# Score tiles by halves of the heads, an earlier second batch, and constants off VectorE, in an attention kernel that feeds a mixture of experts

## The chip, the cores and the metric

The kernel runs on one core of one Trainium2 chip. The metric is the device time of one execution in microseconds (us), the median of several runs. TensorE (PE in the profile) multiplies matrices and writes to PSUM, VectorE (DVE) and ScalarE (ACT) work on tiles element by element, GpSimd (POOL) does the same and issues indirect DMAs, SyncE (SP) issues most of the loads and stores. Each engine takes its own instructions in order and waits on semaphores for the others.

## The reference

Eight batches, eight heads, 512 tokens and 32 states per head, head size 64; then a mixture of eight experts over all 576 rows of a batch, with hidden size 1024.

```python
B, H, S, Ns, D = (8, 8, 512, 32, 64)
scores = scale * np.matmul(x, state.transpose(0, 1, 3, 2))
a = softmax(scores)                          # over the states
xread = np.matmul(a, state)
scores2 = scale * np.matmul(state, x.transpose(0, 1, 3, 2))
a2 = softmax(scores2)                        # over the tokens
sread = np.matmul(a2, x)
x = concat([xread, sread], axis=2)           # to (B, 576, 512)
...
logits = x @ w_gate
local_gate = sigmoid(x @ w_local)
for b, s in rows in order:
    e = argmax(logits[b, s]) if s == 0 or local_gate[b, s] < 0.5 else prev_e
    prev_e = e
    out[b, s] = softmax(logits[b, s])[e] * (relu(x[b, s] @ w1[e]) @ w2[e])
```

Everything is float32 from input to output.

## The kernel before

The kernel has three stages: the attention of the eight batches, the routing (which expert takes which row, and where in the sorted order it goes), and the experts.

In the attention one batch is one round of some 30 steps, each a small method of `Attention`. The steps of all batches are interleaved in one list written out by hand, `STEPS`: a step is two letters and the digits of its arguments (`sc3` is the scores of batch 3, `tr21` a transpose for batch 2, tile 1). They are issued in that order, and each engine runs its own share in that order. `go` ends a piece of the list; the steps behind the first `go` are used as filling between the parts of the routing.

Of a batch, x is held twice: transposed (`x_t0` and `x_t1`, two tiles of 128 x 1024, loaded in two halves by steps `xt`) and with tokens on partitions (`x_n`, step `xn`). Three batches of each fit. The states are held transposed in `sttc` (batch 0 in a tile of its own, batches 1 to 7 in another), and plain in `states_of`, from which four steps `sd` make block-diagonal tiles in `sd`.

Step `sc` (`scores`, L311 to L313) computes the scores of one batch as two PSUM tiles `s`, u = 0 and u = 1, of 128 x 512: on partitions 32k to 32k + 31 of tile u stand the 32 states of head 2k + u. A head takes 64 rows of contraction. So a batch has 8 matmuls of 64 rows x 32 columns x 512 tokens. In before the contraction of tile u lies on partitions 64u to 64u + 63, and k = 0, 1 use `x_t0`, k = 2, 3 use `x_t1`. Behind it: `mx` (maximum over tokens on VectorE), `nb` (scaled on GpSimd), `et` (exponents over tokens on ScalarE), `tr` (32 x 32 transposes of a score tile on VectorE), `mo`, `sb`, `ex`, `zh`, `zs`, `zi`, `ml` (softmax over states, on VectorE, GpSimd and ScalarE), `tb` (turned back on VectorE), `tu` and `ec` (TensorE transposes of the exponents, L383, and their copies), `sr` (state reads, L396), `st`, `rt`, `sl`, `sk` (their logits, L416), `lg` and `lt` (token logits, L428), `vv` (token reads, 2 matmuls each, L438), `xr` and `wr` (copied by ScalarE, L444, and written to the DRAM tensor `rows`, L452). `ga` and `gl` multiply the states with the gate weights (L295). `kp` and `wm` are matmuls on zeros that keep TensorE's clock up (L266, L306).

`Routing.constants` and `Routing.more_constants` make index tables ahead of the attention: iotas on GpSimd, casts on ScalarE, comparisons and memsets on VectorE. `Attention.clear` sets buffers to zero on GpSimd between the two.

The routing begins with the last batch's logits and is mostly one chain on VectorE; the experts multiply by a seven-product scheme on TensorE.

Of the kernel before, what the change touches and what calls it, by code (L numbers as in the profile page):

```python
# [8 lines left out]
F32 = mybir.dt.float32  # L9
I32 = mybir.dt.int32  # L10
BF16 = mybir.dt.bfloat16
# [145 lines left out]
sc0 kp3 xt11 xt10 mx00 ga kp2 sd3 tr01 xt21 mx01 sd2 mo01 nb0 tr00 et01 sb01 xn0 mo00 wm14 sc1 et00 sb00 ex01  # L157
iv0 tu01 tr11 gl tu00 zh01 ex00 tr10 xt20 ec00 zh00 zs01 mo10 sd0 xn1 zs00 sb10 zi0 ec01 mx11 sd1 sr0 ml01 mo11
ex10 mx10 sc2 ml00 st0 xt30 tb01 rt0 sb11 tb00 sl0 xt31 tr20 lg0 nb1 ex11 zh10 sk0 tr21 vv03 et10 zh11 xt41 zs10
vv00 et11 lt0 mx21 xr03 xt51 zs11 tu11 zi1 xr00 tu10 iv1 ml11 mo21 vv02 xt50 ec10 mo20 ml10 sc3 ec11 tb11 xt40  # L160
xr02 mx20 sb21 sr1 tb10 xn2 tr30 sb20 ex21 lg1 mx30 st1 vv12 zh21 ex20 rt1 tr31 nb2 sl1 zh20 et20 vv10 zs21 sk1
lt1 ws1 zs20 et21 tu20 zi2 xt60 mo30 xr10 ml20 sc4 xr12 iv2 mx31 ec20 xn3 ml21 tu21 tb20 vv11 mx41 ec21 nb3 sb30
et30 tb21 sr2 tr40 et31 xt61 lg2 mo31 ex30 tu30 mo40 sb31 st2 sc5 lt2 wr00 xr11 mx40 ec30 zh30 tr41 wr03 tu31
ex31 nb4 zs30 sb40 vv23 et40 mx50 xt70 ec31 mo41 tu40 zh31 ex40 rt2 sr3 sb41 zs31 ws0 xr23 zi3 xn5 et41 iv3 sl2
ml31 mx51 vv22 ex41 sk2 iv4 st3 ml30 tb31 sc6 xr22 rt3 ec40 zh41 tb30 xt71 sl3 zh40 zs41 lg3 tr50 nb5 vv31 wr02
zs40 et50 zi4 vv01 xn4 lt3 xr31 ml40 mo50 sk3 tr51 xr01 vv13 ml41 tb40 et51 vv21 mo51 sb50 xr13 wr10 iv5 vv20
tb41 xr21 sb51 xn6 mx60 ex50 lg4 mx61 xr20 zh50 tu50 ex51 lt4 tu41 tr60 nb6 ec50 zh51 tu51 zs50 et60 mo60 vv32
wr20 ec51 zs51 sb60 zi5 tu60 ec41 wr23 tr61 sc7 xr32 ml50 wr11 ex60 mo61 sr4 et61 ml51 tb50 wr12 mx71 sr5 sb61
ws2 st4 tb51 ec60 ws3 vv30 tr70 zh60 ex61 xn7 mx70 st5 lg5 zh61 xr30 zs60 tu61 mo70 nb7 et70 vv40 zs61 sb70 zi6
ec61 tu70 lt5 wr22 iv6 xr40 ml61 rt5 sr6 rt4 ex70 tr71 wr40 ec70 ml60 mo71 sl5 et71 wr13 sl4 sk5 tb61 vv41 sb71  # L170
st6 wr31 tb60 tu71 zh70 ex71 sk4 iv7 wr32 lg6 rt6 xr41 zs70 zh71 sl6 ec71 lt6 wr21 vv42 zs71 zi7 wr01 sr7 sk6
xr42 ml71 ch0 ch1 wr42 vv33 st7 ml70 wr41 vv50 tb71 xr33 rt7 wr33 sl7 tb70 ch2 xr50 sk7 wr30 wr50 lg7 vv53 xr53 lt7
wr53 vv51 go xr51 wr51 go vv43 xr43 wr43 vv52 xr52 wr52 ws4 go vv61 xr61 wr61 ws5 go vv60 xr60 wr60 vv62 xr62 wr62
vv71 ws7 go xr71 wr71 ws6 go vv72 go xr72 wr72 vv63 xr63 wr63 vv70 xr70 wr70 vv73 xr73 wr73
# [3 lines left out]
class Attention:  # L178


    def __init__(self, ctx, tc, p, late, xn, xt, st, stt, wgl, wgs, lt, rows, none):
# [14 lines left out]
        self.sttc = [once.tile([P, n, KT, N], F32, name=f"sttc{i}") for i, n in enumerate((1, B - 1))]  # L196
# [5 lines left out]
        nc.sync.dma_start(out=self.sttc[1], in_=stt[:, 1:])  # L202
# [82 lines left out]
    def states(self, b):  # L285
        return self.sttc[b > 0][:, b - (b > 0)]

    def gates(self):
        nc = self.nc
        self.ws = [self.bank() for u in range(G)]  # L290
        for u, w in enumerate(self.ws):
            r = slice(64 * u, 64 * u + 64)
            for b in range(B):
                for k in range(KT):
                    nc.tensor.matmul(w[32 * k:32 * k + 32, b * (E + 1):(b + 1) * (E + 1)],  # L295
                                     lhsT=self.states(b)[r, k, :], rhs=self.wh[r, k, :], start=True, stop=True)
# [11 lines left out]
    def scores(self, b):  # L308
        s = [self.new(self.sp, "s", (b, u), [P, S], tag="s") for u in range(G)]
        for k in range(KT):  # L310
            for u in range(G):  # L311
                r = slice(64 * u, 64 * u + 64)
                self.nc.tensor.matmul(s[u][32 * k:32 * k + 32, :], lhsT=self.states(b)[r, k, :],  # L313
                                      rhs=self.get(f"x_t{k // 2}", b)[r, k % 2, :], start=True, stop=True)
# [140 lines left out]
class Routing:  # L455
# [6 lines left out]
    def constants(self, ident):  # L462
# [6 lines left out]

        ci = rt.tile([P, B, NC], I32, name="ci")  # L470
# [14 lines left out]
        self.raw = pi, ci, iof, iob, identb, place  # L485

    def more_constants(self):
        nc, rt = self.nc, self.rt
        pi, ci, iof, iob, identb, place = self.raw
# [4 lines left out]
        before = rt.tile([P, P], BF16, name="before")  # L494
        nc.vector.tensor_scalar(before, iob, part, None, Alu.is_gt)
# [5 lines left out]
        nc.vector.tensor_scalar(ev.rearrange("p e o -> p (e o)"), iof[:, :E], 1.0, None, Alu.add)  # L501
        up = self.up = rt.tile([P, 1, E], F32, name="up")
        nc.vector.tensor_scalar(up[:, 0], iof[:, :E], 1.0, None, Alu.add)
# [862 lines left out]
```

## Time and profile before

| | us |
|---|---|
| median of 3 runs (523.31 to 524.8) | 524.16 |
| the profiled execution | 524.12 |
| its span | 522.3 |
| PE busy | 508.6 (97%) |
| DVE busy | 297.9 (57%) |
| POOL busy | 268.3 (51%) |
| ACT busy | 180.8 (35%) |

The page of the profile lists busy times, then the chain of work that ended last (followed back from the last instruction, at each step to what released it), then groups of instructions with the mean time of one and the idle time ahead of them. A row of a timeline gives start, length, engine, line, operation, `output<-inputs`, sizes and the number of instructions merged in it; in brackets stands the idle time ahead and what ended it. A row of a table of stretches gives its bounds, its length, the busy time of PE, PEld (weight loads), DVE, ACT and POOL with the number of instructions, the granted clock of TensorE, the share of the DMA engines and GB/s. The granted clock is 1.00 in all rows shown here.

### The profile page before, as it was taken

The page shows a single profiled execution, that of the slowest core. Times are in us where ns is not written, and L with a number is a line of the kernel's source. Part 1 is how long each engine was busy: PE and PEld are TensorE (multiplying, and loading weights), DVE is VectorE, ACT ScalarE, POOL GpSimd, SP SyncE. Part 2 cuts the span into 40 slices and gives each one's busy share as a digit, 9 for nine tenths or more (in the row PEclk, how much of TensorE's full clock was granted, in tenths as well). Part 3 has the DMA queues.
Part 4 walks back from the last instruction along what each step waited for, and adds up shares of the span by engine and source line. Part 5 has one row for each costly group of instructions (what it writes and reads, how often), then busy time and mean ns, then how long its engine had stood idle before and what let it go on. Part 6 is the DMA issues. An engine that isn't in the chain of part 4 may idle for free.

```text
span 522.3 us, 10537 instructions
## 1 busy us (share of the span) xinstructions
PE 508.6 (97%) x4028; PEld 423.3 (81%) x4028; DVE 297.9 (57%) x514; ACT 180.8 (35%) x381; POOL 268.3 (51%) x333
## 2 busy tenths in 40 slices
PE   8799999999999999999999999999999999999995
PEld 3557776988888888888888888888888888888884
DVE  5999986989516750684067416661475256715401
ACT  7797755332232322331232222321331232222321
POOL 7788803774663663564474655564554566012002
PEclk9999999999999999999999999999999999999999
DMA  8999777996646815945914964913962947350001
GB/s 318 411 328 399 264 254 217 302 373 232 238 163 214 319 61 207 382 167 178 386 62 139 405 219 142 405 60 124 384 270 73 407 160 229 134 199 25 2 21 67
DMA packets 38142, 116.76 MB, mean 224 GB/s; under 512 B 5425, under 2 KB 6577, under 8 KB 34754
## 3 DMA queue, kind: packets, MB, share of 16 engines
q1 hardware_dynamic: 30866, 98.03, 50.7%
q0 software_dynamic: 7072, 17.90, 10.3%
q8 instruction: 34, 0.56, 0.4%
q14 instruction: 26, 0.21, 0.1%
q10 hardware_dynamic: 144, 0.07, 0.0%
HBM read 98.14 MB, written 17.89 MB: 222 GB/s over the span
## 4 chain that ended last, share of the span: by engine, by line
PE 89%; DMA 4%; DVE 2%; POOL 1%; issue 1%; ACT 1%; SPq 0%; POOLq 0%; DVEq 0%
PE ps L1104 22%; PE ps L1160 21%; PE sum L1104 16%; PE sum L1160 15%; PE p L438 4%; DMA x_t<-in_xt_dram 3%; PE ps L985 3%; PE ps L973 3%; PE s L313 1%; PE p L396 1%; PE p L383 1%; PE ps L735 1%; PE ps L559 1%; DMA y<-rows,four 1%; PE p L428 1%
## 5 line engine op out<-in xcount | busy, mean ns | idle before, releaser
L891 POOL DMA_INDIRECT xg<-rows,row x112 | 126.9, 1133 | 29.6 <-issue 26.5
L1104 PE MATMUL ps<-xt,a 128*128 128x256 f32 (+1 forms) x400 | 91.5, 372 | 0.1
L1104 PE MATMUL sum<-xs,a 128*128 128x256 f32 x376 | 88.7, 379 | 0.0
L1104 PEld LDWEIGHTS ps<-xt,a 128*128 128x128 f32 x400 | 73.3, 190 | 11.3 <-issue 1.8
L1104 PEld LDWEIGHTS sum<-xs,a 128*128 128x128 f32 x376 | 71.4, 190 | 9.7
L1088 POOL DMA_INDIRECT out_dram<-y,tok x32 | 35.1, 1096 | 83.9 <-DVE y L1176 43.6
L999 DVE TENSOR_TENSOR h<-s,s 128x512 f32<-128x512 f32 x16 | 11.1, 695 | 91.2 <-ACT s L1138 91.2
L1160 PE MATMUL ps<-c,h 128*128 128x256 f32 x264 | 63.0, 381 | 0.0
L1160 PE MATMUL ps<-c,hs 128*128 128x256 f32 x256 | 60.5, 379 | 0.0
L904 POOL COPY tick<-s 1x1 f32<-1x1 f32 x72 | 22.9, 318 | 70.5 <-ACT s L1165 45.7
L1160 PE MATMUL sum<-c,h 128*128 128x256 f32 x248 | 58.6, 379 | 0.0
L1160 PEld LDWEIGHTS ps<-c,h 128*128 128x128 f32 x264 | 49.7, 190 | 8.6 <-issue 2.1
L1160 PEld LDWEIGHTS ps<-c,hs 128*128 128x128 f32 x256 | 48.6, 190 | 6.6
L1160 PEld LDWEIGHTS sum<-c,h 128*128 128x128 f32 x248 | 47.1, 190 | 6.4
L999 DVE TENSOR_TENSOR a<-a,a 128x1024 f32<-128x1024 f32 x32 | 37.7, 1215 | 5.8 <-DMA a<-in_w_dram 5.4
L999 DVE TENSOR_TENSOR c<-c,c 128x1024 f32<-128x1024 f32 x32 | 37.6, 1215 | 2.8 <-DMA c<-in_w_dram 2.6
L438 PE MATMUL p<-sd,a 128*128 128x256 f32 x128 | 32.4, 390 | 0.2 <-ACT xr L444 0.2
L1104 PE MATMUL ps<-xs,a 128*128 128x256 f32 x136 | 32.0, 379 | 0.0
L1138 ACT COPY s<-sum 128x512 f32<-128x512 f32 x32 | 18.7, 585 | 37.5 <-PE sum L1104 37.5
L999 DVE TENSOR_TENSOR y<-s,s 128x256 f32<-128x256 f32 x16 | 6.8, 423 | 42.9 <-ACT s L1165 42.9
L1160 PE MATMUL sum<-c,hs 128*128 128x256 f32 x128 | 30.2, 379 | 0.0
L1165 ACT ACTIVATE s<-sum,prob 128x256 f32<-128x256 f32 x32 | 15.2, 474 | 42.7 <-PE sum L1160 42.7
(226 smaller groups left out, 699.7 us busy)
## 6 DMA issues: line engine op xcount, KB each, us to landing
at<-in_w_dram SPq DMA_DIRECT2D x18, 1024.0 KB, 7.7
ct<-in_w_dram SPq DMA_DIRECT2D x18, 1024.0 KB, 10.2
a<-in_w_dram SPq DMA_DIRECT2D x32, 512.0 KB, 5.0
c<-in_w_dram SPq DMA_DIRECT2D x32, 512.0 KB, 10.0
x_t<-in_xt_dram SPq DMA_DIRECT2D x16, 512.0 KB, 11.2
x_n<-in_xn_dram SPq DMA_DIRECT2D x8, 1024.0 KB, 9.6
rows<-xr SPq DMA_DIRECT2D x32, 256.0 KB, 4.4
xg<-rows,row POOLq DMA_INDIRECT x112, 4.7
```

Source lines behind the costliest of these rows:

```text
L313: self.nc.tensor.matmul(s[u][32 * k:32 * k + 32, :], lhsT=self.states(b)[r, k, :], rhs=self.get(f"x_t{k // 2}", b)[r, k % 2, :], start=Tru ...
L438: self.nc.tensor.matmul(v[:, d], lhsT=self.get("a", b, u)[:, c * P:c * P + P], rhs=self.sd[:, b, d], start=True, stop=True)
L891: nc.gpsimd.indirect_dma_start(out=to.rearrange("p x k -> p (x k)"), out_offset=None, in_=rows.rearrange("n q x -> (n q) x"), in_offset=ba ...
L904: nc.gpsimd.tensor_copy(tick, value)
L973: nc.tensor.matmul(hps[SQ * g:SQ * g + SQ, :], lhsT=self.x_t[:, j, :], rhs=a[:, j, :, g], start=(j == 0), stop=(j == KT - 1))
L985: nc.tensor.matmul(yps[SQ * g:SQ * g + SQ, :], lhsT=self.h[:, m, :], rhs=ct_[:, 2 * m // FK, g // 2, m % (FK // 2), g % 2 * P:g % 2 * P + ...
L999: nc.vector.tensor_tensor(out, a, b, op=op)
L1088: put = nc.gpsimd.indirect_dma_start(out=out, out_offset=to, in_=y, in_offset=None, bounds_check=NT - 1, oob_is_err=False)
L1104: nc.tensor.matmul(to[:, m * width + columns.start:m * width + columns.stop], lhsT=w[:, j, f:f + P], rhs=x[:, j, columns], start=begin and ...
L1138: nc.scalar.copy(to, t)
L1160: nc.tensor.matmul(to, lhsT=x[:, m, n * P:n * P + P], rhs=w[:, m, :], start=begin and m == 0, stop=(m == FK // 2 - 1), skip_group_check=True)
L1165: nc.scalar.activation(to, t, Act.Copy, scale=p)
```

## The change

1. **Scores.** Tile u is now computed whole ahead of the other tile, and its contraction uses both halves of the partitions: matmul k of tile u contracts over partitions 64 (k % 2) to 64 (k % 2) + 63 (`heads`). The layouts of `xt`, `stt` and the gate weights in `kernel` follow, so that `x_t0` holds what tile 0 needs and `x_t1` what tile 1 needs. The result in `s` is the same. `gates` uses the same places.
2. **Loads.** `sttc` is three tiles: batch 0, batch 1, batches 2 to 7. Batch 1's states and its x are issued in the constructor, ahead of the other states and the gate weights.
3. **Constants.** The table `before` (1 where the column is greater than the row) is built by GpSimd (`late`) and cast by ScalarE. `ev` is a ScalarE activation and `up` another view of it. `quarter` is four memsets.
4. **First steps.** The first 62 or so steps of the list stand in another order, and `wm14` is gone; from `ex11` on (the last 362 steps) the list is the same.

```diff
-sc0 kp3 xt11 xt10 mx00 ga kp2 sd3 tr01 xt21 mx01 sd2 mo01 nb0 tr00 et01 sb01 xn0 mo00 wm14 sc1 et00 sb00 ex01
...
+sc0 kp4 mx00 tr00 sd3 mx01 nb0 mo00 sc1 kp3 et00 tr01 sb00 mo01 et01 sb01 xn0 xt20 xt21 tu00 tu01 kp2 ga tr10 mx10
...
-        self.sttc = [once.tile([P, n, KT, N], F32, name=f"sttc{i}") for i, n in enumerate((1, B - 1))]
+        self.sttc = [once.tile([P, n, KT, N], F32, name=f"sttc{i}") for i, n in enumerate((1, 1, B - 2))]
...
-        nc.sync.dma_start(out=self.sttc[1], in_=stt[:, 1:])
+        nc.sync.dma_start(out=self.sttc[1], in_=stt[:, 1:2])
+        for h in range(2):
+            self.load_t(1, h)
+        nc.sync.dma_start(out=self.sttc[2], in_=stt[:, 2:])
         nc.sync.dma_start(out=wgs.rearrange("p w k e -> p (w k e)"), in_=wgl)
...
     def states(self, b):
-        return self.sttc[b > 0][:, b - (b > 0)]
+        return self.sttc[min(b, 2)][:, b - min(b, 2)]
+
+    def heads(self, u):
+        return [(slice(32 * k, 32 * k + 32), KT // 2 * u + k // 2, slice(64 * (k % 2), 64 * (k % 2) + 64))
+                for k in range(KT)]
...
     def scores(self, b):
         s = [self.new(self.sp, "s", (b, u), [P, S], tag="s") for u in range(G)]
-        for k in range(KT):
-            for u in range(G):
-                r = slice(64 * u, 64 * u + 64)
-                self.nc.tensor.matmul(s[u][32 * k:32 * k + 32, :], lhsT=self.states(b)[r, k, :],
-                                      rhs=self.get(f"x_t{k // 2}", b)[r, k % 2, :], start=True, stop=True)
+        for u in range(G):
+            for q, k, r in self.heads(u):
+                self.nc.tensor.matmul(s[u][q, :], lhsT=self.states(b)[r, k, :],
+                                      rhs=self.get(f"x_t{u}", b)[r, k % 2, :], start=True, stop=True)
...
+        late = rt.tile([P, P], F32, name="late")
+        nc.gpsimd.memset(late, 0.0)
+        nc.gpsimd.affine_select(out=late, in_=late, compare_op=Alu.is_ge, fill=1.0, base=0, pattern=[[-1, P]],
+                                channel_multiplier=1)
...
+        before = rt.tile([P, P], BF16, name="before")
+        nc.scalar.copy(before, late)
...
-        nc.vector.tensor_scalar(before, iob, part, None, Alu.is_gt)
...
-        nc.vector.tensor_scalar(ev.rearrange("p e o -> p (e o)"), iof[:, :E], 1.0, None, Alu.add)
-        up = self.up = rt.tile([P, 1, E], F32, name="up")
-        nc.vector.tensor_scalar(up[:, 0], iof[:, :E], 1.0, None, Alu.add)
+        nc.scalar.activation(ev[:, :, 0], iof[:, :E], Act.Relu, bias=1.0)
+        self.up = ev.rearrange("p e o -> p o e")
...
-        nc.vector.tensor_scalar(pi, pi, SQ.bit_length() - 1, None, Alu.logical_shift_right)
         quarter = rt.tile([P, 1], F32, name="quarter")
-        nc.vector.tensor_scalar(quarter, pi, float(Q * NT), None, Alu.add)
+        for i in range(Q):
+            nc.vector.memset(quarter[SQ * i:SQ * i + SQ], float(Q * NT + i))
```

How the instructions stand on three engines, at the start of the program. SP's loads before: `x_t_111` and `x_t_113` are the halves of batch 0, `x_t_227` and `x_t_229` of batch 1, `x_t_304` and `x_t_360` of batch 2; batch 0's states come by another queue.

```order
L279 DMA x_t_111<-in_xt_dram 128x1024
L279 DMA x_t_113<-in_xt_dram 128x1024
L201 DMA states_of<-in_st_dram 128x1024
L202 DMA sttc_109<-in_stt_dram 128x896
L203 DMA wgs<-in_wg_dram 128x72
L279 DMA x_t_227<-in_xt_dram 128x1024
L279 DMA x_t_229<-in_xt_dram 128x1024
L279 DMA x_t_304<-in_xt_dram 128x1024
L283 DMA x_n<-in_xn_dram 128x2048
L279 DMA x_t_360<-in_xt_dram 128x1024
```

And SP's loads now: `x_t_112` and `x_t_114` are batch 0, `x_t_119` and `x_t_121` batch 1, `x_t_275` and `x_t_277` batch 2.

```order
L282 DMA x_t_112<-in_xt_dram 128x1024
L282 DMA x_t_114<-in_xt_dram 128x1024
L201 DMA states_of<-in_st_dram 128x1024
L202 DMA sttc_109<-in_stt_dram 128x128
L282 DMA x_t_119<-in_xt_dram 128x1024
L282 DMA x_t_121<-in_xt_dram 128x1024
L205 DMA sttc_110<-in_stt_dram 128x768
L206 DMA wgs<-in_wg_dram 128x72
L286 DMA x_n<-in_xn_dram 128x2048
L282 DMA x_t_275<-in_xt_dram 128x1024
L282 DMA x_t_277<-in_xt_dram 128x1024
```

Batch 1's x has moved ahead of the states of batches 2 to 7 and of the gate weights; in both orders the same tensors stand up to and with batch 2's last half.

TensorE before, from the gates' last matmuls (on `wgs`) over the scores of batch 1 (`x_t_229`, `x_t_227`), batch 0's transposes (`ident`) and state reads (`x_n`) to batch 2's scores and what follows them:

```order
L313 MATMUL s<-x_t_229,sttc_109 32x512 x4
L313 MATMUL s<-x_t_227,sttc_109 32x512 x4
L383 MATMUL p<-ident,e_312 128x128 x4
L383 MATMUL p<-ident,e_336 128x128 x4
L396 MATMUL p<-x_n,e 32x64 x32
L313 MATMUL s<-x_t_360,sttc_109 32x512 x4
L313 MATMUL s<-x_t_304,sttc_109 32x512 x4
L416 MATMUL p<-wgs,rt 32x9 x4
L428 MATMUL p<-a,gl 32x128 x8
```

The same stretch of TensorE now, without the matmuls on zeros between its pieces:

```order
L320 MATMUL s<-x_t_119,sttc_109 32x512 x4
L320 MATMUL s<-x_t_121,sttc_109 32x512 x4
...
L390 MATMUL p<-ident,e_264 128x128 x4
L390 MATMUL p<-ident,e_270 128x128 x4
...
L303 MATMUL p<-wgs,sttc_110 32x9 x24
...
L403 MATMUL p<-x_n,e 32x64 x32
L320 MATMUL s<-x_t_275,sttc_110 32x512 x4
L320 MATMUL s<-x_t_277,sttc_110 32x512 x4
L423 MATMUL p<-wgs,rt 32x9 x4
```

The gates moved from ahead of batch 1's scores to behind batch 0's transposes. A row of four score matmuls was half of the contractions of both tiles, and is one whole tile now.

VectorE before, from the last of the attention's memsets to batch 0's first maximum (`nb<-s`) and transpose:

```order
L495 TENSOR_SCALAR before<-iob,part 128x128
L497 MEMSET ones 128x128
L499 MEMSET one 1x1
L501 TENSOR_SCALAR ev<-iof 128x8
L503 TENSOR_SCALAR up<-iof 128x8
L510 MEMSET on 128x328
L511 MEMSET on 128x8
L518 TENSOR_SCALAR pi<-pi 128x1
L520 TENSOR_SCALAR quarter<-pi 128x1
L522 MEMSET ex 128x40
L321 TENSOR_REDUCE nb<-s 128x1
L340 STREAM_TRANSPOSE e_302<-s 128x512
```

And the same place of VectorE now:

```order
L508 MEMSET ones 128x128
L510 MEMSET one 1x1
L520 MEMSET on 128x328
L521 MEMSET on 128x8
L530 MEMSET quarter 32x1 x4
L532 MEMSET ex 128x40
L328 TENSOR_REDUCE nb<-s 128x1
L347 STREAM_TRANSPOSE e_240<-s 128x512
```

All five operations that read another tile are gone from it; memsets are left.

More of the change, by code (lines that the diff above doesn't have):

```diff
@@ L162 @@
[L162 to L166, printed above, removed]
@@ L175 @@
+wr73
 """
@@ L484, in constants @@
         self.blocks = blocks
-        self.raw = pi, ci, iof, iob, identb, place
+        before = rt.tile([P, P], BF16, name="before")
+        nc.scalar.copy(before, late)
+        self.raw = pi, ci, iof, iob, identb, place, before
     def more_constants(self):
         nc, rt = self.nc, self.rt
-        pi, ci, iof, iob, identb, place = self.raw
+        pi, ci, iof, iob, identb, place, before = self.raw
         part = rt.tile([P, 1], F32, name="part")
@@ L493, in more_constants @@
         nc.scalar.copy(cols, ci.rearrange("p b i -> p (b i)"))
-        before = rt.tile([P, P], BF16, name="before")
-        nc.vector.tensor_scalar(before, iob, part, None, Alu.is_gt)
         ones = rt.tile([P, P], BF16, name="ones")
```

39 lines of the change are left out of this document (21 added, 18 removed).

## The prediction

> **What bounds the kernel now.** I read the page first (TensorE, PE, is busy 97% of the span), then the chain that ended last, then the table of stretches over the attention, then the instructions of TensorE in order of time, and last the start on VectorE (DVE), GpSimd (POOL) and the loads. The change touches nothing behind the attention except constants, so the question is when the attention ends. The chain of work for its first part reads:
>
> ```profile
> 6.65 11.63 DMA x_t<-in_xt_dram
> 18.28 0.04 issue
> 18.32 1.09 PE s L313 x16
> 19.42 0.36 PE p L416 x8
> 19.78 0.13 issue
> 19.91 0.65 PE p L428 x16
> ...
> 24.22 1.02 PE s L313 x16
> ...
> 29.77 1.02 PE s L313 x16
> ...
> 34.30 1.02 PE s L313 x16
> ...
> 38.07 1.38 issue
> ...
> 41.28 1.02 PE s L313 x16
> ```
>
> The columns are start, length and what ran. Until 18.28 us the end hangs on a load, the third batch's transposed x. From there TensorE follows TensorE. The rows of L313 are the score matmuls of batches 2, 3, 4, 5 and 6; those of batch 7 come at 50.89, in this row of TensorE's timeline:
>
> ```profile
> 50.89 1.09 PE L313 MATMUL s<-x_t,sttc 64*32 64x512 f32 x16
> ```
>
> The table of stretches says whether TensorE has room there (length, then the busy time of each engine):
>
> ```profile
> 18.32:38.07 19.75, 19.60 (x347) 12.85 (x348) 19.04 (x45) 16.34 (x40) 15.65 (x22) 1.00 0.98 355
> 38.07:39.45 1.38, 0.00 (x1) 0.00 (x1) 1.12 (x4) 1.29 (x4) 1.38 (x2) 1.00 1.07 423
> 39.45:61.70 22.25, 22.04 (x425) 16.59 (x424) 20.52 (x53) 18.04 (x43) 19.18 (x25) 1.00 0.91 340
> 61.70:72.40 10.70, 10.49 (x130) 7.97 (x131) 9.37 (x27) 5.63 (x12) 2.75 (x3) 1.00 0.70 258
> ```
>
> PE has 19.60 of 19.75 us, then one hole of 1.38, then 22.04 of 22.25. So from 18.3 to 61.7 us TensorE has 0.36 us of room beside that hole. VectorE is close behind (19.04 and 20.52), but TensorE takes its instructions in order, and whatever is added to it there moves everything behind it. That this is work and not modelled ends is seen from what a record costs, below.
>
> **The score tiles (the main term).** In before, the 8 score matmuls of a batch use 8 different places of the array: rows 0-63 for tile u = 0, rows 64-127 for u = 1, and column group k of 32 for each of the four k. After, both tiles use rows 64*(k%2) and columns 32k: the four matmuls of u = 0 occupy four places, and the four of u = 1 the same four again. The other four stand idle. What does that cost? Batch 0 shows four matmuls alone, twice, since the halves of its x land apart:
>
> ```profile
> 5.48:6.60 1.12, 1.06 (x8) 0.15 (x8) 1.00 1.04 424
> 6.60:7.75 1.15, 1.06 (x8) 0.15 (x8) 1.00 1.01 413
> 18.31:19.42 1.11, 1.09 (x16) 0.18 (x16) 1.00 1.00 406
> ```
>
> These are stretches of L313 alone. An f32 matmul leaves two records; 8 records (four matmuls) take 1.06 us, 16 records (eight) take 1.09. So eight places run side by side, and four are no faster than eight. What one place takes follows from the columns streamed through it:
>
> ```profile
> 20.48 1.99 PE L438 MATMUL p<-sd,a 128*128 128x256 f32 x8
> 23.19 1.03 PE L438 MATMUL p<-sd,a 128*128 128x256 f32 x4
> 25.17 1.10 PE L396 MATMUL p<-x_n,e 128*32 128x64 f32 x64
> ```
>
> L438 fills the array: 4 records of 256 columns, 1024 in all, take 1.03 us, and 8 (2048 columns) 1.99. L396 works in four column groups: 64 records / 4 = 16 of 64 columns each, again 1024, 1.10 us. The scores of before put 2 records of 512 = 1024 columns through each place, 1.09 us. After, each of four places gets 4 records of 512 = 2048 columns, which the L438 row prices at 1.99. That is 1.99 - 1.09 = **+0.90 us a batch**; the bounds are 1.99 - 1.10 = 0.89 and 1.99 - 1.03 = 0.96. The trace of before has no row with two matmuls queued on one 64x32 place, so this is an estimate from L396 and L438.
>
> Which batches pay? Batch 0: its halves already run apart, nothing is added. Batch 1 runs before 18.3, where TensorE waits for loads. Batch 2: its first tile needs only the first half of x, which lands one transfer (512 KB by the row below) before the second; at the 406 to 424 GB/s that end the rows of the stretches above that is 0.52/0.41 = 1.3 us, more than the 1.0 that the first tile takes. So only the second tile, 1.06 us, lies behind the last landing, as 1.09 did: nothing. Batches 3 to 7 pay: 5 x 0.90 = **+4.5 us** (4.45 to 4.8).
>
> ```profile
> x_t<-in_xt_dram SPq DMA_DIRECT2D x16, 512.0 KB, 11.2
> ```
>
> **The loads.** Batch 1's x no longer waits for the states of batches 2 to 7 (128 x 768 f32, 393 KB) nor the gate weights (128 x 72, 37 KB): 0.43 MB at some 0.415 MB/us, 1.0 us earlier. But batch 2's x stands behind exactly the same transfers as before, only in another order. The queues are full until then, and the landing that starts the TensorE stretch stays at 18.28. Worth nothing behind 18.3, by itself.
>
> **Constants and first steps.** VectorE begins late today:
>
> ```profile
> 3.31 3.50 POOL L226 MEMSET sd<- 128x4096 f32 x1
> 4.51 2.35 DVE L495 TENSOR_SCALAR before<-iob,part 128x128 bf16<-128x128 bf16 x1 [3.26 <-ACT part L491]
> 4.90 2.48 DVE L503 TENSOR_SCALAR up<-iof 128x8 f32<-128x8 f32 x1
> 7.79 0.69 DVE L321 TENSOR_REDUCE nb<-s 128x1 f32<-128x512 f32 x1
> 13.03 1.31 DVE L340 STREAM_TRANSPOSE e<-s 128x512 f32<-128x512 f32 x2 [0.94 <-PE s L313]
> ```
>
> The two constants wait for ScalarE until 4.51 and then end only when POOL's memset ends at 6.81. They go, and the first maximum need wait only for tile u = 0, which is ready at 5.48 + 1.06 = 6.55: 7.79 - 6.55 = 1.2 us sooner. What is added is hidden: POOL gets two instructions of ident's size ahead of that memset, ScalarE a 128x128 cast and an 8-column activation, all while batch 0 still waits for its maximum. The 1.2 us reach as far as 18.3 us, where x binds. Behind it they can remove only TensorE's small waits for batch 0's state reads and shares: from the end of the scores at 19.34 or so to L428 at 19.91 there are 0.57 us, of which L416 needs 0.36. The gates and their keep-warm matmuls now stand between the scores of batch 1 and the state reads, which takes some of it back. And two copies into `sd` move on ScalarE from ahead of the state reads to behind them:
>
> ```profile
> 16.00 1.04 ACT L274 COPY sd<-states_of 32x1024 f32<-32x1024 f32 x1
> 17.07 0.63 ACT L354 ACTIVATE e<-e 128x512 f32<-128x512 f32 x1
> 18.31 0.52 ACT L402 ACTIVATE ys<-p,i 128x64 f32<-128x64 f32 x2 [0.60 <-PE p L396]
> 19.43 0.63 ACT L354 ACTIVATE e<-e 128x512 f32<-128x512 f32 x1 [0.60 <-POOL e L350]
> ```
>
> Were the state copies (L402) as late as today, the two would end at 18.83 + 2 x 1.04 = 20.9, and the token reads that TensorE begins at 20.48 (L438 above) would wait 0.4 us; the exponents queued behind them on ScalarE hold batch 1's transposes. But the state reads no longer wait for a copy, so they come sooner. I take a gain of 0.1, between -0.4 and 0.36.
>
> **The hole at 38.07.** PE stops in the middle of L396's matmuls with no waker in the profile:
>
> ```profile
> 39.45 0.59 PE L396 MATMUL p<-x_n,e 128*32 128x64 f32 x27 [1.38 <-issue]
> ```
>
> The DMA view of 36.9 to 38.1 us, just ahead of it (packets, MB, share of the 16 engines), and under it the same queue on the page of the whole run:
>
> ```profile
> q1 hardware_dynamic: 199, 0.46, 99.8%
> q8 instruction: 1, 0.02, 4.6%
> ```
>
> ```profile
> q8 instruction: 34, 0.56, 0.4%
> ```
>
> One instruction packet of 0.56 MB / 34 = 16 KB moved there, on engines that the loads hold at 99.8%. If the hole is TensorE waiting for its code, slower scores between the request and the need shorten it; between 0 and all of 1.38. I take half a score's addition, 0.45, since I can't see whether the request falls ahead of batch 5's scores or behind them. The Trainium skill, page "Runtime: NRT & Kernel Launch", section "Instruction fetch mechanics", says that blocks of 16 KiB are fetched while the current one runs, which is mostly hidden; the packet's size agrees, the hole does not look hidden. By that rule the credit would be 0 and the sum 0.45 us higher.
>
> **The sum.** 4.5 - 0.1 - 0.45 = +3.95 us. Does anything behind give it back? Three more pieces of the chain:
>
> ```profile
> 45.07 0.11 ACT xr L444
> ...
> 61.91 1.13 PE p L438 x4
> ...
> 66.35 0.63 PE p L428 x16
> ```
>
> The last one is the last batch's logits. They stand behind all scores on TensorE; the routing's VectorE chain starts from them and the experts follow, so nothing does. The profiled execution took 524.12 us (span 522.3), against a median of 524.16, so both give **528.1 us**. With the bounds: 4.45 - 0.36 - 1.38 = +2.7 and 4.8 + 0.4 = +5.2, so 526.8 to 529.3.
>
> **Rivals.**
> - *Faster: the second tile slips in beside the first.* If the array takes two matmuls for one place as if they were for two, scores stay at 1.09 and the start decides. Then VectorE, busy 19.04 of 19.75, is what counts; batch 2's first tile also comes some 1.3 us sooner, and the 1.2 us of the start are kept: 524.1 - 1.2 = 522.9. For it: VectorE is nearly as full as TensorE. Against it: L396 and L438 both pay for every column on a place. It decides if 16 records of L313 stay under 1.2 us. Chance 0.13.
> - *About the same: the addition is swallowed.* The chain of the end leaves TensorE between 45.07 and 61.91 (rows at the sum) for VectorE, POOL and a row store. If those bind there and batches 6 and 7 cost nothing, and the hole closes fully, 3 x 0.90 - 1.38 - 0.36 = +1.0: 525.1. Against it: TensorE has only 0.21 us of room in 39.45 to 61.70. Chance 0.12.
> - *Much slower: row halves may not share a bank.* In before the two row halves write different PSUM banks; after, both write the bank of the same tile. If they then alternate, each place's four records of a batch wait for the other half's: 4096 columns instead of 2048, another 1.99 a batch, 5 x 1.99 = +10 on top: 538. The Trainium skill, page "TensorEngine Tiling (Array Packing)", section "Restrictions and Gotchas", says that different row tiles can't access one bank at the same time and leaves the order to software; no run here shows it. Against it: they write different partitions, and the rule names no stall. Chance 0.05.
>
> That the change doesn't do what it says I rule out from the order of instructions.
>
> **How the numbers follow.** Forecast 0.70, about 528.1 with its own range 526.8 to 529.3. To hold 8 in 10 the range must reach the two rivals below, and not the far one: 522.5 to 529.6. 0.3% is 1.6 us, about what a measurement can tell from no change. Faster 0.13 is the first rival, same 0.12 the second, slower 0.75 the forecast and the third.
>
> **What would show it.** In the changed profile: 16 records of the score line at 1.9 to 2.0 us in batches 3 to 7 (right) or 1.1 (wrong); TensorE still without holes from 18.3 on; the third batch's x landing at 18.3; the first maximum near 6.6 instead of 7.79; the last logits some 4 us later. The forecast is wrong if scores cost the same, or if TensorE shows holes there that took the addition up.

## The result, and the profile after

The changed kernel takes 530.22 us (median of 4 runs, 529.8 to 531.38), the kernel before on the same chip 524.48 (4 runs, 523.31 to 525.23): a ratio of 1.0100, 95% interval 1.0075 to 1.0126. It is 5.7 us slower. The direction was forecast, the size was not: 528.1 was predicted, and the range ended at 529.6.

The page of the changed kernel begins as follows (busy time, share of the span, instructions). Its profiled execution took 529.8 us, of which the span is 528.0.

```profile
span 528.0 us, 10550 instructions
## 1 busy us (share of the span) xinstructions
PE 515.2 (98%) x4030; PEld 425.3 (81%) x4030; DVE 296.1 (56%) x513; ACT 181.2 (34%) x383; POOL 269.6 (51%) x335
...
PE 93%; DMA 3%; issue 2%; DVE 1%; SPq 0%; POOL 0%; ACT 0%; POOLq 0%; DVEq 0%; ACTq 0%
```

TensorE is busy 6.6 us longer than the 508.6 of before, and VectorE 1.8 us shorter. The chain of work of the changed kernel (start, length, what) shows where:

```profile
14.11 1.21 PE p L303 x89
15.32 0.54 PE p L269 x2
15.86 0.58 PE p L403 x32
16.44 3.67 issue
20.12 1.08 PE p L403 x32
21.20 2.70 PE s L320 x16
...
28.37 1.85 PE s L320 x16
...
34.59 1.85 PE s L320 x16
...
39.95 1.85 PE s L320 x16
...
43.69 1.02 PE p L403 x63
...
45.99 1.85 PE s L320 x16
```

L320 is the score line (L313 in before), L403 the state reads (L396), L303 the gates (L295). The reader is to see three things. The scores of batches 3 to 6 take 1.85 in place of 1.02. The hole that before had at 38.07 in the state reads of batch 3 (batch 2's in two of the expectations below) is gone: 63 of that batch's state reads stand in one piece at 43.69. And a new and longer hole stands at 16.44, in the middle of batch 0's state reads, with "issue" as its reason: nothing that the profile shows holds TensorE back there. The scores behind it last 2.70. The table of stretches says why (bounds, length, busy PE, PEld, DVE, ACT, POOL, granted clock, DMA share, GB/s):

```profile
14.00:16.40 2.40, 2.40 (x163) 1.83 (x163) 2.37 (x6) 1.58 (x4) 2.40 (x3) 1.00 1.03 422
16.44:20.12 3.68, 0.01 (x2) 0.00 (x1) 1.09 (x2) 0.87 (x2) 2.31 (x4) 0.91 1.00 413
20.12:22.84 2.72, 2.72 (x41) 1.23 (x44) 0.31 (x1) 1.57 (x4) 0.00 (x0) 0.50 0.84 342
28.30:30.20 1.90, 1.90 (x21) 0.46 (x24) 1.90 (x4) 0.86 (x3) 1.90 (x3) 1.00 0.89 276
```

In the hole no compute engine is full, only the DMA engines are (share 1.00), and behind it the granted clock of TensorE is 0.50.

**The ledger.** For each TensorE instruction that both kernels have, I took its start after minus its start before, from the two timelines. Growth of this lag is time lost between two rows, a fall is time won:

```
place on TensorE                        start before  after   lag
batch 0's state reads, first record         17.15     15.79   -1.36
batch 0's state reads, last record          18.03     20.88   +2.85
batch 2's scores, last record               18.83     23.31   +4.48
first token reads                           20.48     24.63   +4.15
batch 3's scores: first, last record        24.15     28.30   +4.15, +4.98
batch 4's scores: first, last record        29.70     34.52   +4.83, +5.66
batch 5's scores: first, last record        34.22     39.88   +5.66, +6.49
batch 3's state reads, first record         37.32     43.62   +6.30
batch 3's state reads, last record          39.87     44.50   +4.63  (hole of before)
batch 6's scores: first, last record        41.21     45.92   +4.71, +5.54
batch 7's scores: first, last record        50.89     56.43   +5.54, +6.38
last batch's logits                         66.34     71.76   +5.42
token reads near 78 us                      78.25     83.69   +5.45
```

So +4.15 is lost at the start, five times 0.83 in the scores of batches 3 to 7 (4.15 again), 1.67 comes back where before had its hole, 0.96 between batch 7's scores and the last logits, and 0.26 in small waits between: 4.15 + 4.15 - 1.67 - 0.96 - 0.26 = 5.41, against the 5.42 of the row of the last logits. The rows of the start say where its 4.15 arise: 1.36 is won ahead of batch 0's state reads, 4.21 is lost within them, 1.63 more by the end of batch 2's scores, and 0.33 comes back. Behind the attention the lag stays; the spans differ by 528.0 - 522.3 = 5.7.

**What the new hole is.** Theory: TensorE waits for its code. Counting all records of TensorE from the start of the program, the first as 0 (weight loads, matmuls, and the few waits on semaphores, in order of time), the hole of before ends at record 1217 and the one of after at record 449. These are 193 + 4 x 256 and 193 + 256. A block of 256 records would then be the size of a code packet (34 packets of the queue q8 times 256 is 8704, somewhat above TensorE's 4030 matmuls, 4030 loads and some 130 waits and the like). In after the gates' 256 records run in 1.28 us, and the state reads stand right behind them. The timeline of TensorE:

```profile
14.04 1.28 PE L303 MATMUL p<-wgs,sttc 64*32 64x9 f32 x128
15.79 0.65 PE L403 MATMUL p<-x_n,e 128*32 128x64 f32 x32
20.12 1.08 PE L403 MATMUL p<-x_n,e 128*32 128x64 f32 x32 [3.67 <-issue]
```

The gates enter block 193 at 14.33 us, and 256 records later, at 16.44, TensorE has used it up. The DMA view has no q8 packet from 14.4 to 17.8; in the stretch from 17.8 to 18.85 it has one (packets, MB, share of 16 engines):

```profile
q1 hardware_dynamic: 79, 0.41, 95.4%
q8 instruction: 1, 0.02, 5.8%
```

Rivals: the new score tiles make the hole (L320 begins right behind it, and its second tile uses the first one's places again); or the order of steps does, through some wait that the profile doesn't show.

### The profile page after: what moved, and what is told of

It reads as the page before. It is cut to its first block, busy times and chain, and to the rows that moved or that the text cites. A ratio compares the mean times of both kernels' runs of the same rounds, so it can differ in the third digit from the quotient of the medians.

```text
span 528.0 us, 10550 instructions
## 1 busy us (share of the span) xinstructions
PE 515.2 (98%) x4030; PEld 425.3 (81%) x4030; DVE 296.1 (56%) x513; ACT 181.2 (34%) x383; POOL 269.6 (51%) x335
## 4 chain that ended last, share of the span: by engine, by line
PE 93%; DMA 3%; issue 2%; DVE 1%; SPq 0%; POOL 0%; ACT 0%; POOLq 0%; DVEq 0%; ACTq 0%
PE ps L1114 22%; PE ps L1170 21%; PE sum L1114 15%; PE sum L1170 15%; PE p L445 5%; PE ps L995 3%; PE ps L983 3%; PE s L320 2%; PE p L403 2%; PE p L390 1%; DMA x_t<-in_xt_dram 1%; PE p L435 1%; DMA rows<-xr 1%; DMA y<-rows,four 1%; PE p L423 0%
## 5 line engine op out<-in xcount | busy, mean ns | idle before, releaser
L1009 DVE TENSOR_TENSOR a<-a,a 128x1024 f32<-128x1024 f32 x32 | 37.7, 1216 | 6.9 <-DMA a<-in_w_dram 6.6
```

The lines of the kernel that those rows point to most:

```text
L1009: nc.vector.tensor_tensor(out, a, b, op=op)
```

## The experiments

**1. Scores undone.** The changed kernel with the score and gate matmuls and their layouts as in before. Order, loads and constants stay changed.

```diff
-        for u in range(G):
-            for q, k, r in self.heads(u):
-                self.nc.tensor.matmul(s[u][q, :], lhsT=self.states(b)[r, k, :],
-                                      rhs=self.get(f"x_t{u}", b)[r, k % 2, :], start=True, stop=True)
+        for k in range(KT):
+            for u in range(G):
+                r = slice(64 * u, 64 * u + 64)
+                self.nc.tensor.matmul(s[u][32 * k:32 * k + 32, :], lhsT=self.states(b)[r, k, :],
+                                      rhs=self.get(f"x_t{k // 2}", b)[r, k % 2, :], start=True, stop=True)
```

> The changed kernel with the score and gate matmuls on eight places again (layouts as before); loads, constants and order of steps as changed. Code theory (the 3.67 us hole in batch 0's state reads is TensorE waiting for its next block of 256 instructions, used up fast because the gates' 256 instructions now stand just ahead): the hole stays, 3 to 4 us, ending near 20; the five scores behind it give back 5 x 0.83 = 4.15 us, so 530.2 - 4.2 = 526.0, between 525 and 527.5 (a hole near batch 2's state reads may come back). Rival, the new score tiles make the hole: it is gone, and the time is 524 or less.

Measured: 527.4 us, ratio to before 1.0042 (1.0020 to 1.0063). The hole is where it was, in TensorE's timeline:

```profile
15.85 0.65 PE L405 MATMUL p<-x_n,e 128*32 128x64 f32 x32
20.19 0.68 PE L405 MATMUL p<-x_n,e 128*32 128x64 f32 x32 [3.69 <-issue]
20.80 1.96 PE L322 MATMUL s<-x_t,sttc 64*32 64x512 f32 x16
```

It ends at record 449 again, so the new tiles don't make it. Its lag against before is +3.62 at batch 3's scores, stays there through the scores of batches 3 to 5 (3.62 to 3.46), and falls by 1.63 at the hole of before: without the tiles nothing is added by a batch.

**2. Scores alone.** The kernel before with the new `scores`, `heads`, `gates` and layouts; in the list only `xt11 xt10` and `xt21`, `xt20` change places, since tile 0 now needs `x_t0` alone.

```diff
-sc0 kp3 xt11 xt10 mx00 ga kp2 sd3 tr01 xt21 mx01 ...
+sc0 kp3 xt10 xt11 mx00 ga kp2 sd3 tr01 xt20 mx01 ...
```

> The kernel before with the new score and gate matmuls alone (batch 1's and 2's halves of x exchanged so that the half needed first is loaded first). Code theory: no hole in batch 0's state reads, since the gates stand 8 us ahead of them; 16 score records in 1.9 us from batch 3 on, 5 x 0.83 = +4.15; the 1.38 us hole in batch 2's state reads shrinks or goes: 524.5 + 4.15 - (0 to 1.4) = 527.2 to 528.7. Rival, the new tiles make the hole: 530 or more, with the hole.

Measured: 526.19 us, ratio 1.0030 (1.0005 to 1.0056), some 1 us less than expected. The chain:

```profile
35.99 1.85 PE s L317 x16
37.84 0.59 PE p L387 x4
38.43 0.87 PE p L442 x4
39.29 0.44 PE p L387 x4
39.73 1.02 PE p L400 x63
40.75 0.22 PE p L420 x7
```

There is no hole in the first state reads, and that of before (at 38.07) is gone too. The block from record 961 lasts 6.00 us here, in before 5.41 from its entry to the last record ahead of the hole; and the packet with the next block moves 2.09 us after that entry, in before 4.61. The lag grows by 0.83 a batch from batch 3 on (0.19 to 2.53 behind batch 5), falls by 1.67 at the hole, grows twice more to 2.42, and falls by 0.83 to 1.59 between batch 7's scores and the last logits. That last fall I hadn't expected. Batch 2's scores begin 0.35 us sooner than in before and take 0.83 longer, so batch 2 pays as well.

The lags of experiments 1 and 2 at the last logits, +2.44 and +1.59, make 4.03, and the whole change has +5.42. Most of the difference is the hole of before, which each of them closes by itself (-1.63, -1.67), while together it can be closed only once: 4.03 + 1.65 = 5.68.

**3. Code shifted.** The changed kernel; the ten matmuls on zeros ahead of the first scores become 4 of the same and 72 tiny ones, so that all that follows stands 132 records later.

```diff
-        self.keep(10)
+        self.shift(4, 72)
...
+    def shift(self, n, small):
+        t = self.bank()
+        for i in range(n):
+            self.nc.tensor.matmul(t, lhsT=self.zero[:, :P], rhs=self.zero, start=True, stop=True)
+        for i in range(small):
+            self.nc.tensor.matmul(t[0:1, 0:8], lhsT=self.zero[:, 0:1], rhs=self.zero[:, 0:8], start=True, stop=True)
```

> The changed kernel with six of the first ten keep-warm matmuls replaced by 72 tiny ones, so that everything behind them stands 132 TensorE instructions later in the code; no other edit. Code theory: the boundaries fall on other instructions, the request goes out while TensorE waits for batch 1's x, and the stop in batch 0's state reads after 32 records is gone; what is left is at most 1.2 us, at another place (the gates, or batch 0's token logits): 526 to 528. Rival, a wait on data that the profile does not name: the hole stays after 32 records, 3.7 us, and 530.2 +- 0.7.

Measured: 530.62 us, ratio 1.0097 (1.0061 to 1.0134): no gain, where 526 to 528 was expected. But the timeline shows the hole's place move:

```profile
15.64 0.43 PE L311 MATMUL p<-wgs,sttc 64*32 64x9 f32 x31 [0.42 <-issue]
...
16.54 1.10 PE L411 MATMUL p<-x_n,e 128*32 128x64 f32 x64
...
22.09 0.62 PE L443 MATMUL p<-a,gl 128*32 128x128 f32 x10 [2.01 <-issue]
```

Batch 0's state reads (L411) run whole. Two new holes stand in the middle of two other lines, and the records that end them are again 449 and 705 (193 + 2 x 256). A hole that stays at the record number while the program moves past it is a hole of the code, not of a step. Behind the second one the clock is lower, too:

```profile
22.10:25.90 3.80, 3.80 (x19) 2.90 (x20) 3.08 (x9) 0.94 (x3) 1.39 (x2) 0.64 1.05 426
```

The 0.64 is a mean: the trace has 0.50 from 23.16 to 26.57 us and 1.00 on either side. So the shift lost at and behind the token logits what it won at the state reads. The expectation named both places, but with 1.2 us at most; there are two holes, together 2.43 us, and the lower clock. The edit also takes six long matmuls out of the start, where batch 0's scores now take 3.64 us in place of 2.16.

**4. Gates sooner.** The changed kernel with step `ga` right behind `sc1`, so that its 256 records no longer stand right ahead of the state reads.

```diff
-... sc1 kp3 et00 tr01 sb00 mo01 et01 sb01 xn0 xt20 xt21 tu00 tu01 kp2 ga tr10 mx10
+... sc1 ga kp3 et00 tr01 sb00 mo01 et01 sb01 xn0 xt20 xt21 tu00 tu01 kp2 tr10 mx10
```

> The changed kernel with the gate matmuls moved from behind batch 0's transposes to right behind batch 1's scores, some 2 us sooner, the same instructions otherwise. Code theory: the request goes out at about 12.4 instead of 14.3, the code is there 5.8 us later: the hole in the state reads ends near 18.2 instead of 20.1 and is 1.8 to 2.4 us long, and TensorE's clock may stay up: 527 to 528.7. Rival, a wait on data: the hole still ends at 20.1, and 530.2 +- 0.7.

Measured: 527.18 us, ratio 1.0047 (1.0023 to 1.0070), 3.0 us under the changed kernel. TensorE's timeline, and the stretch behind the hole:

```profile
16.20 0.65 PE L403 MATMUL p<-x_n,e 128*32 128x64 f32 x32
18.44 0.65 PE L403 MATMUL p<-x_n,e 128*32 128x64 f32 x32 [1.58 <-issue]
19.02 1.92 PE L320 MATMUL s<-x_t,sttc 64*32 64x512 f32 x16
```

```profile
18.44:20.90 2.46, 2.46 (x49) 0.93 (x49) 1.03 (x2) 1.73 (x4) 0.13 (x1) 1.00 1.01 413
```

The same instructions with the same score tiles: the block before is entered 1.85 us sooner (12.48), the hole ends 1.68 sooner, and behind it the clock stays at 1.00. The lag at batch 3's scores is +1.44, in place of +4.15. This is the cheapest repair of the change, and two thirds of what it lost at the start.

**5. First steps undone.** The changed kernel with the first steps in before's order (batch 1's x stays in the constructor).

```diff
-sc0 kp4 mx00 tr00 sd3 mx01 nb0 mo00 sc1 kp3 et00 tr01 sb00 mo01 et01 sb01 xn0 xt20 xt21 tu00 tu01 kp2 ga tr10 mx10
...
+sc0 kp3  mx00 ga kp2 sd3 tr01 xt20 mx01 sd2 mo01 nb0 tr00 et01 sb01 xn0 mo00 wm14 sc1 et00 sb00 ex01
...
```

> The changed kernel with its first 62 steps in the order of before (gates ahead of batch 1's scores again, 14 keep-warm matmuls instead of two groups); scores, loads and constants as changed. Code theory: the gates' code is entered near 12 us (when the gate weights land), so the next block comes near 18 and stops the state reads for about 1 us instead of 3.67, and the clock stays up: 526.5 to 528, close to the scores alone (526.2). Rival, the loads or the constants make the start late: the hole or another wait stays and the time is 529 or more.

Measured: 530.99 us, ratio 1.0116 (1.0093 to 1.0139), a miss. No hole of the code is left, yet the timeline has another wait:

```profile
12.11 1.28 PE L303 MATMUL p<-wgs,sttc 64*32 64x9 f32 x128 [3.12 <-DMA wgs<-in_wg_dram]
13.31 0.78 PE L269 MATMUL p<-zero 128*128 128x512 bf16 x2
13.89 1.91 PE L314 MATMUL s<-zero 128*128 128x512 bf16 x4
15.73 2.53 PE L320 MATMUL s<-x_t,sttc 64*32 64x512 f32 x16
```

With batch 1's x loaded ahead of the gate weights, gates that stand ahead of batch 1's scores wait 3.12 us for those weights, and behind the wait TensorE is slow (the granted clock is 0.65 from 13.31 to 18.20, and four matmuls on zeros take 1.91). Batch 1's scores, 11.83 in before, begin at 15.73. So the new order of loads needs the gates behind batch 1's scores, and the order of steps as it was given put them too far behind.

**6. Before, shifted by 152 records.** The edit of experiment 3 in the kernel before, `shift(4, 82)`.

> The kernel before, with six of its ten first keep-warm matmuls replaced by 82 tiny ones: all TensorE code stands 152 instructions later, nothing else. Code theory: each 256 instructions then last 6.5 us or more where the loads are dense (5.6 us at the hole of 38.07 today), so that hole goes or is under 0.4 us: 523.0 to 524.0, against 524.5. Rival, the hole is something else: still 1.38 us at 38.07 and 524.5 +- 0.5.

Measured: 528.53 us, ratio 1.0064 (1.0039 to 1.0088): slower, a miss. The profiled run is the longest of its seven (533.11), so its losses are larger than those of the median. The hole at 38.07 is gone but for 0.23 us at record 1217, and new losses take its place. Behind 4 matmuls on zeros in place of 10 TensorE is slower at the start: three matmuls on zeros take 1.46 us in place of 0.82, and batch 1's scores, at 15.76, still 1.96 in place of 1.09. The table of stretches prints a granted clock of 1.00 there, but the trace's first record of the clock comes at 18.08 us (at 5.36 in before), so that 1.00 isn't a measurement. Two holes stand elsewhere, at records 449 and 1473 (193 + 5 x 256). The first of them, and what stands ahead:

```profile
5.72 3.01 PE L321 MATMUL s<-x_t,sttc 64*32 64x512 f32 x16 [0.53 <-DMA sttc<-in_stt_dram]
8.67 1.46 PE L266 MATMUL p<-zero 128*128 128x512 bf16 x3
10.06 1.66 PE L303 MATMUL p<-wgs,sttc 64*32 64x9 f32 x118
12.77 0.38 PE L303 MATMUL p<-wgs,sttc 64*32 64x9 f32 x10 [1.05 <-issue]
```

**7. Old scores, gates sooner, shifted by 168 records.** Experiments 1 and 4 together, with `shift(4, 90)`: this leaves of the change its loads, its constants and its order but for `ga`.

> Loads and constants of the change, scores on eight places as before, the gates right behind batch 1's scores, and the code shifted by 168 instructions so that the block boundary that falls into the gates is asked for before 7 us. Code theory: no hole over 0.4 us between 12 and 62 us; batch 2's x (18.3) starts the TensorE stretch as in before, without before's hole at 38.07: 522.5 to 524.0, faster than both kernels. Rival, holes aren't set by block boundaries: a hole of 1 us or more in the state reads, 526 or more.

Measured: 524.85 us, ratio 0.9999 (0.9985 to 1.0013), slightly above what was expected. One hole of 0.43 us is left in its profile (record 705). The whole loss is gone, and nothing is won. What loads, constants and order bring by themselves isn't measured here, since the shift slows the start: batch 0's state reads begin at 17.48 us, in before at 17.15.

**8. Before, shifted by 64 records**, `shift(8, 34)`, which keeps 8 of the 10 matmuls on zeros, and **9. old scores and gates sooner without a shift.** Both ran on a chip on which all runs were some 12 us longer and more scattered (before: 536.57).

> The kernel before, with two of its first ten keep-warm matmuls replaced by 34 tiny ones: TensorE's code stands 64 instructions later, and the first matmuls stay as long as they were. Code theory: the 256 instructions up to the next boundary then last 6.0 to 7.7 us everywhere between 9 and 50 us, where today the ones that end in the hole of 38.07 last 5.6; no hole over 0.5 us there: 523.0 to 524.0 against 524.6. If the code comes late at 24 to 30 us instead, a hole stands exactly at another multiple of 256 and the time is 524 to 525. Rival: the hole stays at 38.07 in batch 2's state reads, 524.6 +- 0.4.

> The run with old scores, sooner gates, loads and constants of the change, but without its shift of the code: what loads and constants are worth when neither the scores nor a clocked-down TensorE hide it. Code theory: the hole of 1.6 us in batch 0's state reads of the run with sooner gates alone, ending at 18.4, just as batch 2's x lands; then eight-place scores: between 523.5 and 525.5, within 0.2% of before. If loads and constants carried a gain past 18.3 us it would be 523 or less.

Measured: 538.17 us, ratio 1.0044 (1.0007 to 1.0081), and 537.43 us, ratio 0.9982 (0.9945 to 1.0018). Experiment 8 is a miss in time. Its hole of before is 0.58 us long, at record 1217 again, though the code moved by 64 records under it, and 1.63 us are lost ahead of that batch's state reads. Experiment 9 agrees with 7: its interval, -3.0 to +1.0 us, tells no difference from before. The run that was profiled took 543.01 us; it has holes of 1.64 us at record 449 and of 1.57 at record 1217. No version tried beats the kernel before.

**All holes together.** For each hole of 0.4 us or more in the attention that has no waker and stands in the middle of a group, and the code packet ahead of it, from the traces:

```
kernel     record   block before    packet moves     TensorE     packet's end
                    entered (us)    (us)             resumes     to resuming
before     1217       32.44         37.05 - 37.93     39.45        1.52
after       449       14.33         17.83 - 18.81     20.12        1.31
exp. 1      449       14.39         17.90 - 18.87     20.19        1.32
exp. 3      449        9.79         13.37 - 14.39     15.64        1.25
exp. 3      705       15.64         19.71 - 20.66     22.09        1.43
exp. 4      449       12.48         16.14 - 17.10     18.44        1.34
exp. 6      449        6.81         10.31 - 11.34     12.77        1.43
exp. 6     1473       38.16         44.86 - 45.87     47.17        1.30
exp. 7      705       14.12         17.71 - 18.67     20.02        1.35
exp. 8     1217       31.59         37.33 - 38.22     39.83        1.61
exp. 9      449       12.55         16.18 - 17.14     18.57        1.43
exp. 9     1217       33.84         38.95 - 39.83     41.20        1.37
```

Every one ends 1.25 to 1.61 us behind the end of a code packet, and every one at a record 193 + 256 n, in nine kernels. With the shift of experiment 3 that is what I call shown: these holes are TensorE waiting for its next block of 256 instructions. From entering the block before to resuming it takes 5.8 to 7.4 us, in two cases 8.2 and 9.0. Where the packet comes in time, there is no hole: in after, records 961 to 1216 last from 38.08 to 44.05 (5.97 us), the packet for record 1217 comes at 40.08 to 40.96, and the state reads run through.

The Trainium skill, page "Runtime: NRT & Kernel Launch", section "Instruction fetch mechanics", names blocks of 256 instructions in 16 KiB. The record numbers agree. It calls the cost of crossing into a block mostly hidden; the 3.67 us of after and the 1.38 of before, on the path of TensorE, say otherwise for bursts of short matmuls.

What stays open is why the packet moves only some 3.5 us after the block before is entered (4.6 in before, 6.7 in experiment 6). The loads hold the DMA engines at 95 to 104% at these places, which suggests a queue. Other blocks of the same traces fit: in experiment 3 the packet behind the block entered at 31.30 comes after 0.37 us with idle DMA engines (share 0.00), in after the one behind 59.65 after 0.67 us (share 0.17). But in after the one behind 38.08 also comes after 2.00 us at a share of 0.98, so busy engines alone don't give the delay. No run took the loads away, and the moment of the request isn't in the trace.

## Why the prediction was wrong

**The step that failed is the start**, "I take a gain of 0.1, between -0.4 and 0.36". Measured: +4.15 at batch 3's scores. I had counted what moves in instructions and waits, and had the gates in sight ("The gates and their keep-warm matmuls now stand between the scores of batch 1 and the state reads, which takes some of it back"), but gave them no price of their own, and not that of the 256 instructions of code that they are. The thought that TensorE may wait for its code stood in the prediction, but only for the old hole at 38.07; it was not put to the place that the gates moved to. So a wait was missing from that term, and not only its size was off. Experiment 4 prices their place: with `ga` sooner the lag is +1.44, so 2.71 of the 4.15 come from where the gates stand, the longer hole and the halved clock behind it. In the other 1.44 are the hole of 1.58 that is left there and batch 2's scores, less what the earlier start gives.

**Batch 2 pays too.** I took it that its second half of x lands when the first tile is done, so that only one tile lies behind. In after the 16 records run behind the hole without a wait for x, and take 2.70 at half clock. At full clock (experiments 2 and 4) they take 1.92, 0.83 more than before. So the landing at 18.28 did not set the pace any more: in experiment 2 the scores begin at 17.97, when the state reads ahead of them are through, and the first tile can't run ahead of that.

**The score tiles.** Mechanism right, size a little off: 1.92 for 16 records in place of 1.09, +0.83 a batch and not +0.90; 4.15 for batches 3 to 7, where 4.5 was forecast (bounds 4.45 to 4.8). The timeline of after has the same row in all five, of which two:

```profile
28.30 1.92 PE L320 MATMUL s<-x_t,sttc 64*32 64x512 f32 x16
...
56.43 1.92 PE L320 MATMUL s<-x_t,sttc 64*32 64x512 f32 x16
```

The rival by which two matmuls on one place cost nothing is out (1.92, not 1.2). So is the one by which the two row halves of a tile take turns on their bank, which would have made it 1.99 more: four places worked side by side on one bank. On this the Trainium skill, page "TensorEngine Tiling (Array Packing)", section "Restrictions and Gotchas", and the trace differ: different row tiles did write one bank at the same time, to different partitions, with no time lost.

**The hole at 38.07.** The guess at its cause holds, by the record numbers. The credit was too small: 0.45 was taken, and 1.67 came back, more than the bound of 1.38 (from the last state read ahead of the hole, at 37.85, to the first behind it, at 39.45, before lost 1.60). And slower scores, the reason for the credit, aren't needed: experiment 1 closes the hole too (-1.63) with the old scores, and its block from record 961 lasts 5.28 us. Its packet moves 2.83 us after the block is entered, that of experiment 2 2.09 and that of after 2.00, where before has 4.61. Experiment 9, also with the old scores, has 5.11 and keeps a hole of 1.57. So the hole closed mainly because the packet came sooner, and why it did is open.

**"So nothing does" give it back.** Wrong by 0.96. The lag falls from +6.38 to +5.42 between batch 7's scores and the last logits, in experiments 2 and 4 as well (2.42 to 1.59, 3.67 to 2.72). There TensorE of before has small waits that a later TensorE no longer meets. One of them, in the timelines of before and of after:

```profile
61.27 0.41 PE L416 MATMUL p<-wgs,rt 128*32 128x9 f32 x8
61.91 1.13 PE L438 MATMUL p<-sd,a 128*128 128x256 f32 x4 [0.22 <-ACT xr L444]
```

```profile
67.19 0.40 PE L423 MATMUL p<-wgs,rt 128*32 128x9 f32 x8
67.51 1.13 PE L445 MATMUL p<-sd,a 128*128 128x256 f32 x4
```

From start to start it is 0.64 us before and 0.32 after, so 0.32 comes back there, of which before's timeline shows 0.22 as idle. I had taken the room from the busy shares (0.21 us of 22.25, 0.21 of 10.70), in which the modelled ends of matmuls cover part of such waits. So the rival of the swallowed addition was right in a small part: about one fifth of the 4.15.

**Loads and constants.** Batch 1's scores begin at 9.83 in place of 11.83, but only the first tile does, which now needs one half of x. The second begins at 10.99, when the other half is there, 0.84 us sooner than before's scores, where 1.0 was worked out for the loads. The first maximum on VectorE waits for one tile only, as said:

```profile
7.04 0.69 DVE L328 TENSOR_REDUCE nb<-s 128x1 f32<-128x512 f32 x1 [4.69 <-PE s L320]
```

It comes at 7.04, not 6.6, since batch 0's first score begins at 5.91 in place of 5.49. In after the hole swallows the 1.36 us that batch 0's state reads are ahead by; whether any of it could reach the end isn't shown, since experiment 7 slows its own start and the interval of experiment 9 is wide. The copies into `sd` cost nothing in after: at the token reads the lag falls from 4.48 to 4.15. But the wait of 0.4 us that the prediction feared for them is real where the scores are short. In experiment 9's timeline the copies end at 21.78, and TensorE is idle for 0.80 us ahead of the token reads that need them (the view names no waker):

```profile
19.70 2.08 ACT L277 COPY sd<-states_of 32x1024 f32<-32x1024 f32 x2
...
21.89 1.96 PE L447 MATMUL p<-sd,a 128*128 128x256 f32 x8 [0.80 <-issue]
```

With the measured sizes in the forecast's own form: +4.15 for the start, +4.15 for the scores, -1.67 for the hole, -0.96 behind and -0.26 in between make +5.4, and another 0.3 is lost behind the attention (5.7 in the spans). That the forecast is only 2.1 us off is luck in part: the start was wrong by +4.25, and the scores (-0.35), the hole (-1.22) and the end (-0.96) were wrong the other way.

## What to carry to other kernels

Count instructions as well as time: a burst of many tiny matmuls (128 of the gates with 128 weight loads in 1.28 us) uses up a block of code, and where another burst followed here, the engine stood still until the next block was there, some 6 us or more after it had entered the block before. A step that moves takes its code along, so a hole with no waker is first checked by the record number at which it ends, in both kernels. An order of steps and an order of loads belong together, and a tile layout for a 64-row contraction should keep all eight places of the array in use, or each batch pays 0.83 us here.

## What the runs showed of the hardware that was not expected

- TensorE's code came in blocks of 256 records; twelve holes in nine kernels ended 1.25 to 1.61 us behind a 16 KB packet.
- In six kernels the trace has a granted clock of 0.50 for 3.4 us at or behind an idle time of TensorE: 3.67 us (after), 3.69 (experiment 1), 2.01 (3), 3.12 (5), 1.78 (6) and 2.72 (8). Idle times of 3.21 us (before), 2.14 (2), 1.64 (9) and 1.58 (4) left it at 1.00. So the length of the idle time alone doesn't decide. The one of before, in its timeline:

```profile
17.15 1.10 PE L396 MATMUL p<-x_n,e 128*32 128x64 f32 x64 [3.21 <-ACT sd L274]
```

- At the start of experiment 6 TensorE took 1.46 us for what takes 0.82 elsewhere, and the trace holds no record of the clock ahead of 18.08 us: a granted clock of 1.00 in a table says nothing where no record stands.
